# A hand-ordered first batch in a fused relu² attention and ReGLU feed-forward kernel: a relu, three gates, an exchange and some matmul passes change places

## The chip, the cores and the metric

The kernel runs on one core of one Trainium2 chip. The metric is the device time of one execution in microseconds (us). Before the change it is 420.81 us, the median of three runs (419.86 to 421.45). One more execution was taken with the hardware profiler; all durations below are from that one.

## The reference

Eight batches, 12 heads, 448 positions, head size 64; all inputs and the output are float32.

```python
scores = (1/8) * q @ k.transpose(0, 1, 3, 2)          # per batch and head: 448 x 448
attn   = np.maximum(scores, 0) ** 2 / 448
x      = (attn @ v)                                   # to 3584 tokens x 768 (heads side by side)
out    = (np.maximum(x @ w_gate, 0) * (x @ w_val)) @ w_out   # 768 -> 1536 -> 768
```

The kernel computes in bfloat16 with float32 accumulation. All constant factors are put into the scale of the gate's relu.

## The kernel before, in words

**Engines.** TensorE (PE) does every product as groups of four 64x64 matmuls that work side by side, one *pass* (`mm4`, L80) of 448 columns. ScalarE (ACT) and VectorE (DVE) read the results in PSUM. GpSimd (POOL) does little but issue loads and stores; SyncE (SP) issues DMA transposes and a few stores. Every instruction is pinned to program order (`pin`), so each engine works through its own queue in exactly the order in which the kernel text issues. An instruction that waits holds all that stand behind it on its engine.

**PSUM.** Eight banks, used in pairs. Score tiles and values take pairs 0 and 2 (`sc_later`, L193) or, in the first batch, 0, 2 and 4 in turn (`sc_first`). The FFN's sums take pairs 6 and 4 (`acc`). The first two FFN units of batch 0 have buffers of their own (`BEGUN_IN`, L349): pair 4 and pair 2. A buffer can be written again only when what read it is done.

**One batch of attention.** 21 score tiles, numbered n, seven for each of three *quads* of four heads (`tile_of`, L235). A tile is one pass. `relu2` (L223) then takes its 128x896 result: a relu on ACT from PSUM into a bfloat16 buffer `r_sb` (four buffers; L225), and a square on DVE (L226) into `attn`. When a quad's seven tiles are squared, seven *value passes* make its part of x (`value_passes`, L244), which is copied to x0. `exchange` (L251) then swaps the two halves of the partitions from x0 into x1, by two DVE copies.

**FFN.** `gv_unit` (L273): for each 128 of the 1536 hidden columns (index mf), 12 passes over x0 (e = 0) and x1 (e = 1), then a gate relu on ACT (L291) and a product on DVE (L292) into `hT`. `out_unit` (L309): 12 passes, added up and stored. From the second batch on, the score tiles of the next batch are laid between the passes of the FFN by hand-given places (unit, step) in `spread` and `evenly` (L458 to L472); three `transposes_event`s turn batch 1's q and k.

**The first batch** has no FFN to stand beside, and `first_batch` (L380) writes its order out by hand: some idle matmuls on zeros, the transposes of head pairs 0 and 1 (`first_transposes`), then the tiles. At n = 3, 5, 7, 9 two idle matmul pairs and the transposes of one more head pair follow the tile, each with a DVE copy from PSUM (`transposes`, L202); quad 1 needs head pairs 2 and 3. A tile's relu and square are issued two tiles later (`scored`). The values of quad 0 and 1 come after tile 12 and 17, with one DVE copy to x0 each (L415). Eight FFN passes (four for mf 0, four for mf 1) are done ahead of the last values; then come the exchanges, the copy of quad 2's x by ACT (L428), and the last 16 passes of mf 0 and 1. The regular FFN begins with mf 2.

**Loads** are all issued on POOL's queue, in the order of L363 to L376; a load is issued when the one eight places before it has landed. mf 0 and 1 use the weight chunk `gv0`, mf 2 to 5 `gv1`.

**End.** `out_pieces` (L330) writes the last 128 rows in three pieces, with their stores on the queues of POOL (2), SP (2), then ACT and SP (1 each), as L344 lists them.

Of the kernel before, what the change touches and what calls it, by code (L numbers as in the profile page):

```python
# [11 lines left out]
AF = mybir.ActivationFunctionType  # L12
# [4 lines left out]
def kernel(  # L17
# [22 lines left out]
    nc = tc.nc  # L40
# [28 lines left out]
    def pin(ins):  # L69
        return tc.keep_in_program_order(ins)  # L70
# [112 lines left out]
    def rotation(numbers):  # L183

        turn = [0]

        def take():
            n = numbers[turn[0] % len(numbers)]
            turn[0] += 1
            return banks[:, n:n + 2, :]  # L190
        return take

    sc_first, sc_later, acc = rotation((0, 2, 4)), rotation((0, 2)), rotation((6, 4))  # L193

    def transposes(b, hp, bank):

        ps = bank.bitcast(BF16).rearrange("p (t c) -> p t c", t=2)
        for t, nat in enumerate((kn_b[b % NB], qn_b[b % NB])):
            for i in range(4):
                for h2, half in HALVES:  # L200
                    pin(nc.tensor.transpose(ps[half, t, i * 128:i * 128 + 128], nat[:, 2 * hp + h2, i, :], ident))  # L201
        pin(nc.vector.tensor_copy(T_b[b % NB][:, :, hp, :], ps[:, :, 0:S]))  # L202
# [17 lines left out]
        for c in range(2):  # L220
            transposes(b, pair_of(b, 2 * qd + c), ps[:, c, :])

    def relu2(src, dst):  # L223
        r = rpool.tile([128, 2, S], BF16, name="r_sb")
        pin(nc.scalar.activation(r, src, AF.Relu))  # L225
        pin(nc.vector.tensor_tensor(dst, r, r, ALU.mult))  # L226

    attns = {}
# [1 line left out]
    def attn_of(b, qd):  # L230
        if (b, qd) not in attns:
            attns[b, qd] = atpool.tile([128, 2 * NC, S], BF16, name="attn")
        return attns[b, qd]

    def tile_of(b, n, ps):  # L235

        qd, i = divmod(n, NC)
        T = T_b[b % NB]
        a = i * 128 if i < 4 else (i - 4) * 128 + 64
        mm4([ps[:, r, :S] for r in range(2)], lambda r, c: T[:, 0, pair_of(b, 2 * qd + c), a:a + 64],  # L240
            lambda r, c: T[:, 1, pair_of(b, 2 * qd + c), :], True, True)
        return ps[:, :, :S], attn_of(b, qd)[:, 2 * i:2 * i + 2, :]

    def value_passes(b, qd, ps, i0, i1):  # L244

        attn, v_sb = attn_of(b, qd), v_b[b % NB]
        for i in range(i0, i1):
            mm4([ps[:, r, :S] for r in range(2)], lambda r, c: v_sb[:, 2 * qd + c, i, :],
                lambda r, c: attn[:, 2 * i + c, :], i == 0, i == NC - 1)

    def exchange(b, qd):  # L251
        a = slice(2 * qd, 2 * qd + 2)
        for (_, p), (_, other) in zip(HALVES, HALVES[::-1]):
            pin(nc.vector.tensor_copy(x_of[b][1][p, a, :], x_of[b][0][other, a, :]))  # L254

    def values(b, qd, ps):
        value_passes(b, qd, ps, 0, NC)
# [4 lines left out]
    def idle_matmuls(ps, n):  # L262

        for _ in range(n):
            mm2(ps[:, :S], blank[:, 0:128], blank, True, True)
# [4 lines left out]
    def new_x(b):  # L270
        x_of[b] = [xpool.tile([128, HP, S], BF16, name=f"x{n}") for n in range(2)]

    def gv_unit(b, mf, order, take):  # L273

        hT = hT_of[b - b % 2]
        c0 = CHUNK_OF[mf]
        w = gv_sb[c0]
        f = mf * 128 - CHUNKS[c0][0]
        col = (b % 2) * S
        o = []  # L280

        def step(n, e, hp):
            if n == 0:
                ps = take()
                o.extend(ps[:, r, :S] for r in range(2))
            x = x_of[b][e]
            mm4(o, lambda r, c: w[:, 2 * pair_of(b, hp) + (r ^ e), f + c * 64:f + c * 64 + 64], lambda r, c: x[:, hp, :],
                n == 0, n == H - 1)
            if n == H - 1:
                g_sb = gpool.tile([128, S], BF16, name="g_sb")  # L290
                pin(nc.scalar.activation(g_sb, o[0], AF.Relu, scale=float(out_scale)))  # L291
                pin(nc.vector.tensor_tensor(hT[:, mf, col:col + S], o[1], g_sb, ALU.mult))  # L292
        return [lambda n=n, e=e, hp=hp: step(n, e, hp) for n, (e, hp) in enumerate(order)]

# [9 lines left out]
    def store(b0, t, o_sb, c0, c1, engines):  # L304
        for s in range(2):
            pin(engines[s].dma_start(out=segment_rows(b0, 2 * t + s)[:, c0:c1],  # L306
                                     in_=o_sb[s * 64:s * 64 + 64, c0:c1]))
# [22 lines left out]
    def out_pieces(b0, t):  # L330

        hT = hT_of[b0]
        o_sb = opool.tile([128, d_model], FP32, name="o_sb")
        cuts = [0, OH, OH + OH // 2, d_model]
        turn = [acc(), acc()]
        for n, (c0, c1) in enumerate(zip(cuts, cuts[1:])):
            o_ps = turn[n % 2][:, n // 2, :c1 - c0]
            for kf in range(KF):
                mm2(o_ps, hT[:, kf, bass.ts(t, 128)], wo_sb[kf // 6][:, kf % 6, c0:c1], kf == 0, kf == KF - 1)
            if n == 2:  # L340
                pin(nc.vector.tensor_copy(o_sb[:, c0:c1], o_ps))  # L341
            else:
                pin(nc.scalar.activation(out=o_sb[:, c0:c1], in_=o_ps, func=AF.Copy))
            store(b0, t, o_sb, c0, c1, ((nc.gpsimd, nc.gpsimd), (nc.sync, nc.sync), (nc.scalar, nc.sync))[n])  # L344

    STRAIGHT = [(e, hp) for e in range(2) for hp in range(HP)]

    BEGUN = [(e, 2 * qd + c) for qds in (range(0, 2), range(2, 3)) for e in range(2) for qd in qds for c in range(2)]
    BEGUN_IN = (4, 2)  # L349

    def gv_units(b):
        b0 = b - b % 2
# [27 lines left out]
    def first_batch(units):  # L380


        def passes(u, n):
            for _ in range(n):
                units[u].pop(0)()

        def bank(n):
            return banks[:, n, :]

        def tile(n, at=None):  # L390
            todo.append(tile_of(0, n, sc_first() if at is None else banks[:, at:at + 2, :]))

        todo = []

        def scored():
            relu2(*todo.pop(0))

        idle_matmuls(bank(6), 12)
        first_transposes((6, 7, 5, 4))
        idle_matmuls(bank(2), 4)  # L400
        tile(0)
        tile(1)
        both = banks[:, 6:8, :]
        for n in range(2, 19):
            tile(n)
            if n in (3, 5, 7, 9):
                hp = n // 2 + 1
                idle_matmuls(bank(6 + hp % 2), 2)
                transposes(0, hp, bank(6 + hp % 2))
            if n in (12, 17):  # L410
                value_passes(0, n // 14, both, 0, NC)
            scored()
            if n in (12, 17):
                qd = n // 14
                pin(nc.vector.tensor_copy(x_of[0][0][:, 2 * qd:2 * qd + 2, :], both[:, :, :S]))  # L415
        tile(19)
        scored()
        passes(0, 4)
        scored()
        tile(20, 0)  # L420
        scored()
        value_passes(0, 2, both, 0, 4)
        scored()
        passes(1, 4)
        value_passes(0, 2, both, 4, NC)
        exchange(0, 0)
        exchange(0, 1)
        pin(nc.scalar.activation(x_of[0][0][:, 4:6, :], both[:, :, :S], AF.Copy))  # L428
        exchange(0, 2)
        for n in range(4):  # L430
            for u in range(2):
                passes(u, 2)

    def scores_event(b, n):
        return lambda: relu2(*tile_of(b, n, sc_later()))

    def values_event(b, qd):
        return lambda: values(b, qd, sc_later())

    def transposes_event(b, qd):  # L440
        return lambda: transpose_quad(b, qd)
# [16 lines left out]
    def spread(units, events):  # L458

        events = sorted(events, key=lambda e: e[:2])  # L460
        for u, unit in enumerate(units):
            for n, step in enumerate(unit):
                while events and events[0][:2] <= (u, n):
                    events.pop(0)[2]()
                step()
        assert not events

    def evenly(units, u0, u1, events):

        at = [(u, n) for u in range(u0, u1) for n in range(len(units[u]))]  # L470
        places = [at[int((i + 0.5) * len(at) / len(events))] for i in range(len(events))]
        return [(u, min(n, len(units[u]) - 4), e) for (u, n), e in zip(places, events)]  # L472
# [10 lines left out]
    units = units[2:] + [first[:8] + second[:8] + first[8:] + second[8:]] + more + out_units(0) + out_units(1)  # L483
    last = len(units) - 1
    todo = events_of(1)
    spread(units, [(2, 6, transposes_event(1, 0)), (2, 6, transposes_event(1, 1)), (2, 10, transposes_event(1, 2)),
                   (3, 0, todo.pop(0)), (10, 1, todo.pop())] + evenly(units, 3, 10, todo) +
           [(10, 7, values_event(1, 2)), (11, 0, lambda: new_x(2)),
            (13, 0, lambda: dma_transposes(2, 0)), (14, 6, lambda: dma_transposes(2, 1)),
            (19, 0, lambda: (hold(2), load_qk(3), load_v(3))), (last, 2, values_event(2, 2))] +  # L490
           evenly(units, 20, last - 1, events_of(2)) +
# [41 lines left out]
```

## Time and profile before

| what | us |
|---|---|
| median of three runs | 420.81 |
| the profiled execution | 420.87 |
| its span, first to last instruction | 419.1 |
| PE busy | 409.0 (98%) |
| DVE busy | 241.8 (58%) |
| ACT busy | 236.5 (56%) |
| relu of a score tile on ACT, 168 | 0.922 each |
| square on DVE, 168 | 0.624 each |
| gate relu on ACT, 96 | 0.543 each |
| exchange copy on DVE, 48 | 0.388 each |

The busy share of PE is an average. In the page's 40 slices of 10.5 us, PE has 7 and 8 tenths in the first two, in the second of which ACT has 9 and DVE 8; from the third on PE has 9 in all but the last, which has 5. A row of the timeline gives the start, the time from the first start to the last end, the engine, the line, what is written and read, and how many instructions were merged ("x8"); in brackets stands the idle time of the engine before it and what ended it.

### The profile page before, as it was taken

Reading aid. Unit: us, or ns where it says so; the run is one execution under the profiler, and the core shown is the slowest. Engines: PE = TensorE matmul, PEld = TensorE weight load, DVE = VectorE, ACT = ScalarE, POOL = GpSimd, SP = SyncE. Lnnn points to the kernel's source line nnn. Section 1 sums busy time; section 2 is a strip of 40 time slices with the busy share of each in tenths; the row PEclk is TensorE's granted clock in tenths of the full one; section 3 lists DMA queues with packets and bytes.
Section 4 is the critical chain, followed back from the end, with each engine's and each line's share of the span. In section 5 each row is a group of like instructions: output and inputs, shape, how many; then the busy total and the mean of one; then the engine's idle time right before and its main releaser. Section 6 shows DMA issues by size and latency. Waiting matters only on the chain.

```text
span 419.1 us, 19286 instructions
## 1 busy us (share of the span) xinstructions
PE 409.0 (98%) x8856; PEld 351.6 (84%) x8856; DVE 241.8 (58%) x424; ACT 236.5 (56%) x345; POOL 89.5 (21%) x147
## 2 busy tenths in 40 slices
PE   7899999999999999999999999999999999999995
PEld 3467677789989998899988999899988999889984
DVE  4885885437765766557555666556655565642221
ACT  4961884247765665565664756656665756622221
POOL 7923510024226100250023400260011000010012
PEclk9999999999999999999999999999999999999999
DMA  9999999359956960399323991289403100130014
GB/s 154 170 202 196 200 208 176 69 75 183 223 114 115 176 123 2 78 174 137 66 50 90 179 134 40 62 127 167 97 21 98 41 2 4 39 80 3 2 42 115
DMA packets 84338, 44.34 MB, mean 106 GB/s; under 512 B 54304, under 2 KB 82496, under 8 KB 84256
## 3 DMA queue, kind: packets, MB, share of 16 engines
q0 software_dynamic: 49600, 34.19, 52.6%
q1 hardware_dynamic: 34304, 8.67, 13.3%
q8 instruction: 69, 1.13, 1.1%
q10 hardware_dynamic: 352, 0.25, 0.2%
q14 instruction: 13, 0.11, 0.1%
HBM read 47.19 MB, written 11.01 MB: 139 GB/s over the span
## 4 chain that ended last, share of the span: by engine, by line
PE 93%; DVE 3%; DMA 1%; POOL 1%; ACT 1%; issue 0%; POOLq 0%; ACTq 0%
PE ps L73 92%; DVE attn L226 2%; DMA qn<-in_q_dram 1%; DVE kqT L202 1%; PE ps L201 1%; ACT r_sb L225 1%; POOL qn L116 0%; POOL kn L116 0%; DVE x L415 0%; DVE hT L292 0%; ACT g_sb L291 0%; DVE o_sb L341 0%; POOL ident L112 0%; POOLq L112 0%; ACTq L225 0%
## 5 line engine op out<-in xcount | busy, mean ns | idle before, releaser
L73 PE MATMUL ps<-x,gv 64*64 64x448 bf16 x4608 | 242.8, 349 | 0.7 <-ACT r_sb L225 0.3
L73 PEld LDWEIGHTS <-gv 64*64 64x64 bf16 x4608 | 193.8, 107 | 30.3 <-issue 2.7
L225 ACT ACTIVATE r_sb<-ps 128x896 bf16<-128x896 f32 x168 | 151.4, 922 | 51.0 <-PE ps L73 45.7
L226 DVE TENSOR_TENSOR attn<-r_sb 128x896 bf16<-128x896 bf16 x168 | 103.7, 624 | 77.7 <-ACT r_sb L225 77.0
L73 PE MATMUL ps<-wo,hT 64*64 64x384 bf16 (+2 forms) x2664 | 124.8, 321 | 0.2 <-issue 0.2
L73 PEld LDWEIGHTS <-hT 64*64 64x64 bf16 (+1 forms) x2664 | 105.5, 107 | 11.8 <-issue 1.1
L292 DVE TENSOR_TENSOR hT<-ps,g_sb 128x448 bf16<-128x448 f32 x96 | 59.7, 622 | 50.4 <-ACT g_sb L291 49.6
L291 ACT ACTIVATE g_sb<-ps 128x448 bf16<-128x448 f32 x96 | 52.1, 543 | 64.7 <-PE ps L73 60.7
L306 POOL DMA_DIRECT2D out_dram<-o_sb x56 | 29.7, 536 | 263.5 <-DVE o_sb L325 262.3
L73 PE MATMUL ps<-kqT 64*64 64x448 bf16 x672 | 75.7, 351 | 2.6 <-ACT r_sb L225 2.1
L73 PEld LDWEIGHTS <-kqT 64*64 64x64 bf16 x672 | 34.2, 107 | 9.3 <-issue 4.2
L325 DVE TENSOR_TENSOR o_sb<-ps,o_sb 128x384 f32<-128x384 f32 x54 | 29.9, 554 | 18.3 <-ACT o_sb L324 18.2
L324 ACT ACTIVATE o_sb<-ps 128x384 f32<-128x384 f32 x54 | 26.4, 488 | 24.8 <-PE ps L73 24.3
L73 PE MATMUL ps<-attn,vn 64*64 64x448 bf16 x672 | 38.6, 350 | 0.0
L73 PEld LDWEIGHTS <-vn 64*64 64x64 bf16 x672 | 28.5, 107 | 4.4 <-issue 0.3
L116 POOL DMA_DIRECT2D vn<-in_v_dram x36 | 23.8, 701 | 19.4 <-PE ps L73 8.0
L258 ACT ACTIVATE x<-ps 128x448 bf16<-128x448 f32 x21 | 11.4, 543 | 28.4 <-PE ps L73 28.4
L259 DVE CAST x<-ps 128x448 bf16<-128x448 f32 x21 | 13.1, 625 | 14.3 <-PE ps L73 14.3
L254 DVE COPY x<-x 64x896 bf16<-64x896 bf16 x48 | 18.6, 388 | 2.7
L116 POOL DMA_DIRECT2D qn<-in_q_dram x20 | 14.6, 761 | 1.1 <-POOLq L517 0.8
L116 POOL DMA_DIRECT2D kn<-in_k_dram x16 | 12.2, 776 | 0.8 <-DVE attn L226 0.5
L73 PE MATMUL ps<-blank 128*64 128x448 bf16 x48 | 7.4, 447 | 1.2 <-DVE blank L88 1.2
(35 smaller groups left out, 57.8 us busy)
## 6 DMA issues: line engine op xcount, KB each, us to landing
out_dram<-o_sb POOLq DMA_DIRECT2D x54, 192.0 KB, 3.6
kn<-in_k_dram POOLq DMA_DIRECT2D x7, 384.0 KB, 5.9
qn<-in_q_dram POOLq DMA_DIRECT2D x7, 384.0 KB, 8.3
vn<-in_v_dram POOLq DMA_DIRECT2D x14, 192.0 KB, 10.1
wo<-in_moe_w_out_dram POOLq DMA_DIRECT2D x2, 1152.0 KB, 16.8
kn<-in_k_dram POOLq DMA_DIRECT2D x7, 288.0 KB, 7.0
qn<-in_q_dram POOLq DMA_DIRECT2D x7, 288.0 KB, 9.9
vn<-in_v_dram POOLq DMA_DIRECT2D x14, 144.0 KB, 10.2
```

Source lines behind the costliest of these rows:

```text
L73: pin(nc.tensor.matmul(o, lhsT=l, rhs=r, start=start, stop=stop, skip_group_check=True))
L116: pin(nc.gpsimd.dma_start(out=o, in_=i))
L225: pin(nc.scalar.activation(r, src, AF.Relu))
L226: pin(nc.vector.tensor_tensor(dst, r, r, ALU.mult))
L254: pin(nc.vector.tensor_copy(x_of[b][1][p, a, :], x_of[b][0][other, a, :]))
L258: pin(nc.scalar.activation(x_of[b][0][:, 2 * qd, :], ps[:, 0, :S], AF.Copy))
L259: pin(nc.vector.tensor_copy(x_of[b][0][:, 2 * qd + 1, :], ps[:, 1, :S]))
L291: pin(nc.scalar.activation(g_sb, o[0], AF.Relu, scale=float(out_scale)))
L292: pin(nc.vector.tensor_tensor(hT[:, mf, col:col + S], o[1], g_sb, ALU.mult))
L306: pin(engines[s].dma_start(out=segment_rows(b0, 2 * t + s)[:, c0:c1], in_=o_sb[s * 64:s * 64 + 64, c0:c1]))
L324: pin(nc.scalar.activation(state[t][:, m], o[0], AF.Copy))
L325: pin(nc.vector.tensor_tensor(state[t][:, m], o[1], state[t][:, m], ALU.add))
```

## The change

- **A relu on DVE.** Tile 1's relu moves from ACT to DVE (`tensor_scalar_max`, from PSUM). It stays where it was issued: after tile 3, the transposes of head pair 2 and their copy.
- **Values sooner.** The values of quad 0 come after tile 11 (was 12), of quad 1 after tile 16 (was 17).
- **An exchange by DMA.** Quad 0's exchange is two DMAs on SP's queue, issued right after its copy to x0.
- **A third score buffer.** Tiles up to 14 take pairs 0, 2, 4 in turn; from tile 15 on they take 0 and 2, so that pair 4 is free for mf 0 from tile 17 on. mf 1 takes pair 0. Twelve FFN passes are done ahead of the last values, not eight: two after tile 17, two after tile 18, four after the first values of quad 2, and four more after tile 20's relu.
- Quad 2's copy to x0 is split between ACT and DVE; two idle matmul pairs after `first_transposes`, not four.
- **Gates.** In batch 0 the gate relus of mf 6, 8 and 10 move to DVE.
- **Places.** Batch 1's transposes and tiles begin later in the FFN of batch 0 and are spread over six units, not seven.
- **Last stores.** The second store of the second piece moves from SP to POOL.

```diff
-    def relu2(src, dst):
+    def relu2(src, dst, engine=nc.scalar):
         r = rpool.tile([128, 2, S], BF16, name="r_sb")
-        pin(nc.scalar.activation(r, src, AF.Relu))
+        if engine is nc.scalar:
+            pin(nc.scalar.activation(r, src, AF.Relu))
+        else:
+            pin(engine.tensor_scalar_max(r, src, 0.0))
         pin(nc.vector.tensor_tensor(dst, r, r, ALU.mult))
...
-            pin(nc.vector.tensor_copy(x_of[b][1][p, a, :], x_of[b][0][other, a, :]))
+            new, old = x_of[b][1][p, a, :], x_of[b][0][other, a, :]
+            pin(nc.vector.tensor_copy(new, old) if queue is None else queue.dma_start(out=new, in_=old))
...
-                pin(nc.scalar.activation(g_sb, o[0], AF.Relu, scale=float(out_scale)))
+                if b == 0 and mf >= 6 and mf % 2 == 0:
+
+                    pin(nc.vector.tensor_scalar(out=g_sb, in0=o[0], scalar1=float(out_scale), scalar2=0.0,
+                                                op0=ALU.mult, op1=ALU.max))
+                else:
+                    pin(nc.scalar.activation(g_sb, o[0], AF.Relu, scale=float(out_scale)))
...
-            store(b0, t, o_sb, c0, c1, ((nc.gpsimd, nc.gpsimd), (nc.sync, nc.sync), (nc.scalar, nc.sync))[n])
+            store(b0, t, o_sb, c0, c1, ((nc.gpsimd, nc.gpsimd), (nc.sync, nc.gpsimd), (nc.scalar, nc.sync))[n])
...
-    BEGUN_IN = (4, 2)
+    BEGUN_IN = (4, 0)
...
+        def buffer_of(n):
+            at = 2 * (n % 3) if n < 15 else 2 - 2 * (n % 2)
+            return banks[:, at:at + 2, :]
...
+        def scored(n):
+            relu2(buffer_of(n)[:, :, :S], attn_part(0, n), nc.vector if n == 1 else nc.scalar)
...
-        idle_matmuls(bank(2), 4)
+        idle_matmuls(banks[:, 2, :], 2)
         tile(0)
         tile(1)
-        both = banks[:, 6:8, :]
-        for n in range(2, 19):
+        for n in range(2, 17):
             tile(n)
             if n in (3, 5, 7, 9):
                 hp = n // 2 + 1
-                idle_matmuls(bank(6 + hp % 2), 2)
-                transposes(0, hp, bank(6 + hp % 2))
-            if n in (12, 17):
-                value_passes(0, n // 14, both, 0, NC)
-            scored()
-            if n in (12, 17):
-                qd = n // 14
-                pin(nc.vector.tensor_copy(x_of[0][0][:, 2 * qd:2 * qd + 2, :], both[:, :, :S]))
+                idle_matmuls(banks[:, 6 + hp % 2, :], 2)
+                transposes(0, hp, banks[:, 6 + hp % 2, :])
+            if n in (11, 16):
+                values_of(n // 16)
+            scored(n - 2)
+            if n in (11, 16):
+                copied(n // 16)
+            if n == 11:
+                exchange(0, 0, nc.sync)
+        scored(15)
+        tile(17)
+        passes(2, 0)
+        scored(16)
+        tile(18)
+        passes(2, 0)
+        scored(17)
         tile(19)
-        scored()
-        passes(0, 4)
-        scored()
-        tile(20, 0)
-        scored()
+        scored(18)
+        tile(20)
+        scored(19)
         value_passes(0, 2, both, 0, 4)
-        scored()
-        passes(1, 4)
+        passes(4, 1)
+        scored(20)
+        passes(2, 0, 1)
         value_passes(0, 2, both, 4, NC)
-        exchange(0, 0)
         exchange(0, 1)
-        pin(nc.scalar.activation(x_of[0][0][:, 4:6, :], both[:, :, :S], AF.Copy))
+        pin(nc.scalar.activation(x_of[0][0][:, 4, :], both[:, 0, :S], AF.Copy))
+        pin(nc.vector.tensor_copy(x_of[0][0][:, 5, :], both[:, 1, :S]))
         exchange(0, 2)
-        for n in range(4):
-            for u in range(2):
-                passes(u, 2)
+        for _ in range(3):
+            passes(2, 0, 1)
...
-    spread(units, [(2, 6, transposes_event(1, 0)), (2, 6, transposes_event(1, 1)), (2, 10, transposes_event(1, 2)),
-                   (3, 0, todo.pop(0)), (10, 1, todo.pop())] + evenly(units, 3, 10, todo) +
-           [(10, 7, values_event(1, 2)), (11, 0, lambda: new_x(2)),
+    spread(units, [(3, 4, transposes_event(1, 0)), (3, 4, transposes_event(1, 1)), (3, 8, transposes_event(1, 2)),
+                   (3, 10, todo.pop(0)), (10, 2, todo.pop())] + evenly(units, 4, 10, todo) +
+           [(10, 8, values_event(1, 2)), (11, 0, lambda: new_x(2)),
```

`passes(n, u, ...)` now takes n passes from each named unit in turn; `values_of` and `copied` are the two steps that stood in the loop.

## The prediction

> **What bounds the kernel now.** I read the page first, for the engine that is full:
>
> ```profile
> PE 409.0 (98%) x8856; PEld 351.6 (84%) x8856; DVE 241.8 (58%) x424; ACT 236.5 (56%) x345; POOL 89.5 (21%) x147
> PE   7899999999999999999999999999999999999995
> ```
>
> PE is full from the third slice on, so an edit pays only if it takes work from PE, closes gaps in PE's first 30 us, or shortens the tail behind the last matmul. A busy row hides short gaps, because an isolated pass is drawn 0.38 us long and back to back passes start 0.19 us apart (16 matmuls, four passes, last 0.95). So I read PE's waits in the first batch next, the window from 8 to 28 us:
>
> ```profile
> PE ps L73 <- ACT r_sb L225: 2.5, 6, 0.6
> ACT r_sb L225 <- PE ps L73: 0.9, 2, 0.8
> ```
>
> PE waits for ACT's relus, and ACT hardly waits: its chain of relus is the bound there. The timeline shows its pace, and the place where the change cuts in:
>
> ```profile
> 10.79 0.41 PE L201 MATMUL ps<-ident,qn 128*64 128x128 bf16 x8 [0.42 <-DMA qn<-in_q_dram]
> 11.13 0.57 PE L73 MATMUL ps<-kqT 64*64 64x448 bf16 x8
> 11.24 0.62 DVE L202 COPY kqT<-ps 128x896 bf16<-128x896 bf16 x1 [1.37 <-PE ps L201]
> 11.78 1.15 DVE L226 TENSOR_TENSOR attn<-r_sb 128x896 bf16<-128x896 bf16 x2
> ...
> 19.17 1.09 DVE L415 CAST x<-ps 128x896 bf16<-128x896 f32 x1
> ```
>
> The reader is to see three things. Head pair 2's q lands near 10.7; the transposes and their DVE copy follow. Tiles 4 and 5 start on PE at 11.13, at once. And DVE's square of tile 1 waits behind that copy until 11.78. ACT's starts, from narrow windows: tile 4 at 11.57, tile 20 at 24.93, mostly 0.80 apart; 16 steps of 0.80 are 12.8 of those 13.36 us, so 0.56 is gaps.
>
> **Step 1: tile 1's relu on DVE, the deciding one.** ACT has one relu fewer: -0.80 on its chain, if nothing else moves. But DVE's queue has the new relu behind head pair 2's copy, so it starts at 11.78. No row shows a relu on DVE. Its nearest row is the copy from the same float32 PSUM shape, 1.09 (L415); the low end is 0.62 (L202, 896 elements of bfloat16). I take 1.09: done at 12.87. Tile 4 writes pair 2, which tile 1 held (4 and 1 have the same rest by 3), and in the changed order its first matmul waits for DVE. It starts at 12.92 instead of 11.13, **+1.79** (low end +1.3). Queued behind it on PE are tile 5, the idle pairs, head pair 3's transposes and tile 6. ACT, done with tile 3 near 10.8, has nothing until 12.92 + 0.43 (tile 0: PE at 7.86, ACT at 8.29) = 13.35, against 11.57: **+1.78**. From tile 4 on ACT has the same 17 relus as before. So the one saved lies ahead of the hole, where it saves nothing. The two idle pairs left out (4 matmuls, 0.37) also lie ahead of it: 0, the DMA covers them.
>
> **Step 2: from the relus to mf 2.** With the same gaps (bounds 0 and twice 0.56) all relus come 1.8 later. Tile 18's starts at 23.33 before (two steps of 0.80 ahead of 24.93), so at 25.13, and ends at 26.05; tile 20 needs its buffer and starts at 26.10. From there PE has tile 20, 4 value passes, 4 FFN, 4 FFN, 3 value passes and 12 FFN: 28 x 0.19 = 5.32, so mf 2 starts at 31.42, plus about 0.2 for the last square and exchanges. Before, mf 2's gate started at 33.00, so its last pass at 32.57 and its first, 11 x 0.19 earlier, at 30.48. Difference **+1.1**, which has the four passes begun sooner in it (-0.76) and the DVE exchanges that no longer stand at the end:
>
> ```profile
> 26.71 2.48 DVE L254 COPY x<-x 64x896 bf16<-64x896 bf16 x6
> ```
>
> PE had some 0.5 of waits there. Bounds +0.5 (0.62 relu, all gaps closed, less the four passes) and +1.9 (the begun passes win nothing). Values one tile sooner, and the split copy of quad 2: 0, since ACT's chain ends later than they do; if that cover went, they would save parts of the same 0.5.
>
> **Step 3: exchange by DMA.** Quad 0's copy ends near 21 (after tile 11 instead of 12, -0.8, in a chain +1.8, from 20.26). SP starts the second DMA 0.83 later, as its last three stores are spaced. Landing after issue: 2.3 (the stores), 4.6 (SP's first k load, beside other loads), 5.9 (SP transposes at 103 to 117 us beside loads): 24.1 to 27.7. Its readers stand 9 passes behind tile 20, at 27.8. I take 0. Its 0.23 MB at some 190 GB/s delay the loads by 1.2: `gv1` lands at 28.7 (the load eight places later is issued then), so 29.9, still ahead of mf 2 at 31.4; batch 1's q at 36.2, so 37.4, ahead of its transposes, which move back by some 20 passes.
>
> **Step 4: mf 2 to mf 13.** 19 tiles and two values lie over 6 units instead of 7. Per unit PE needs 12 x 0.19 + 3.2 x 0.19 + 14/6 x 0.19 = 3.3. ACT needs 3.2 x 0.80 + half a gate (three of six move) 0.27 + copies 0.18 = 3.0; DVE 3.2 x 0.55 + 0.62 + half a gate at 0.63 (L259) 0.31 + values and exchange 0.47 = 3.2. PE still ends last, narrowly. Its waits there, read as steps beyond 0.19, are some 1.2 us before; I take 0, bounds -0.5 (the transposes no longer meet a load that lands at 36.15) and +0.7 (DVE blocks once per unit).
>
> **Step 5: the tail.**
>
> ```profile
> 414.02 2.16 SPq L306 DMA_DIRECT2D out_dram<-o_sb  x3
> 414.66 0.36 DVE L341 COPY o_sb<-ps 128x192 f32<-128x192 f32 x1 [3.10 <-PE ps L73]
> 415.04 0.54 ACTq L306 DMA_DIRECT2D out_dram<-o_sb  x1
> ```
>
> SP's third store starts at 415.66 only because two stand ahead of it; with one ahead it starts when DVE is done, 415.07: -0.59. POOL's added store starts at 414.5 and lands by 417.7 at the slowest row (3.2), against 417.9 before. I take **-0.4** (bounds -0.6, -0.1).
>
> **Sum.** +1.1 + 0 + 0 - 0.4 = +0.7, and +0.1 for the first-batch gaps, which I expect a little wider: +0.8. The profiled execution took 420.87 (span 419.1 and 1.77 around it), 0.06 over the median of the runs. Forecast **421.7**, no measurable change by the bound of 0.5% (2.1 us), about what a measurement of this kernel can tell from none. Bounds together: -0.6 and +2.5, so 420.2 to 423.3.
>
> **A rule and a row on the clock.** After the last matmuls the granted clock falls:
>
> ```profile
> 414.00:417.00 3.00, 0.61 (x16) 0.40 (x10) 0.36 (x1) 0.00 (x0) 0.50 (x1) 1.00 0.63 181
> 417.00:419.00 2.00, 0.00 (x0) 0.00 (x0) 0.00 (x0) 0.00 (x0) 0.00 (x0) 0.69 0.05 12
> ```
>
> It held for about 3 us without matmuls and then fell. PE's new hole, from 11.13 to 12.92, is 1.8 us; PE's longest hole before in the batch was about 0.9, at a clock of 1.00. The Trainium skill, "TensorE: Matmul & The Clock Gate", Part 1, has the clock halve after an idle window of about 3.4 us; by that the hole is short enough, and the trace agrees with its size.
>
> **Rivals.**
>
> *A: slower, the exchange DMA comes late.* It shares the DMA engines with loads that are queued deep: batch 1's k and q, issued at 15.8 to 18, took 14.7 to 17.9 to land. If the exchange needs over 6.0 from its issue at 21.8, PE stands still at 27.8 with everything behind it. At 8 us: +2.0, so **423.7**; at 14.7, +8.7. For: DMA is at 9 tenths there. Against: SP's own transfers beside loads landed in 4.6 and 5.9. The Trainium skill, "DMA: Bandwidth & Descriptors", Queues, rings and completion order, says that a DMA engine takes queues in turn, packet by packet; by that rule the deep queue doesn't hold the exchange, which no run here shows yet. Chance 0.15.
>
> *B: slower, the clock falls in the hole.* A window that is already partly idle (PE is sparse from 8 us) could end inside it. Then the next 3.4 us run at half pace: tiles, idle pairs and transposes of some 2.6 us take 5.2 where ACT needs 3.2, +2.0: **423.7**. Chance 0.05.
>
> *C: faster, the hole isn't paid.* If tile 1's relu were done before tile 4 needs it, ACT's chain would end 0.8 sooner, the four passes and the exchange would win up to 0.76, the tail 0.4: **418.9**. That is what the edit says it does. It speaks against this that the DVE queue holds the relu behind a copy that waits for a DMA; even a landing 2 us sooner leaves square, copy and relu in line (9.24 + 0.55 + 0.54 + 1.09 = 11.4). Chance 0.10.
>
> **How the numbers follow.** Forecast 0.70, A 0.15, B 0.05, C 0.10. Over 0.5% faster (below 418.7) is half of C: 0.05. Over 0.5% slower (above 422.9) is A, B and the forecast's upper end, 0.05: 0.25. Same: 0.70. The range takes the bounds, and reaches into A and B and towards C: 419.7 to 424.0.
>
> **What would show it.** In the changed trace: a gap on PE up to about 12.9 that ends with the DVE relu, and one on ACT from 10.8 to 13.3 (step 1); the last tile's relu near 26.7 and mf 2's gate near 34 (step 2); SP's exchange landing before 27.8, and no PE wait for it (step 3; else A); PE waits of about 1.2 us from 31 to 72 (step 4); SP's last store at some 0.6 after the one before it ends, and a span end 4.0 rather than 4.4 after the last matmul (step 5); a clock of 1.00 from 8 to 30 (else B). Wrong would be: no hole at tile 4, a DVE relu much under 1 us, or ACT or DVE becoming the bound in step 4.

## The result, and the profile after

The changed kernel takes 422.43 us (median of ten runs, 421.6 to 423.95), the kernel before 420.46 beside it: ratio 1.0047, 95% interval 1.0031 to 1.0063, so about 2.0 us slower, inside the bound of 0.5%. The profiled execution took 423.24 (span 421.4), 2.37 more than that of before. Its page, first lines and slices of PE:

```profile
span 421.4 us, 19282 instructions
PE 409.7 (97%) x8852; PEld 348.3 (83%) x8852; DVE 244.0 (58%) x427; ACT 233.6 (55%) x341; POOL 90.0 (21%) x148
PE   8799999999999999999999999999999999999995
```

PE's busy time grew by 0.7 us only, so most of the 2.3 us by which the span grew is idle time. I looked for it in the three places where PE has gaps. The first is the first batch; PE's waits there, from 8 to 28 us (total, times, longest):

```profile
ACT r_sb L226 <- PE ps L73: 2.7, 3, 2.0
PE ps L73 <- ACT r_sb L226: 2.1, 4, 0.6
PE ps L73 <- DVE r_sb L228: 1.7, 1, 1.7
```

The last row is new: one wait of 1.7 us for a relu on DVE (L228). The timeline around it:

```profile
10.78 0.62 DVE L202 COPY kqT<-ps 128x896 bf16<-128x896 bf16 x1 [0.76 <-PE ps L201]
11.32 1.08 DVE L228 TENSOR_SCALAR r_sb<-ps 128x896 bf16<-128x896 f32 x1
12.45 0.57 PE L73 MATMUL ps<-kqT 64*64 64x448 bf16 x8 [1.72 <-DVE r_sb L228]
12.93 2.54 ACT L226 ACTIVATE r_sb<-ps 128x896 bf16<-128x896 f32 x3 [1.96 <-PE ps L73]
```

DVE's relu stands behind head pair 2's copy; PE starts tile 4 when it is done (this is the hole of step 1), and ACT, idle for 1.96 us, follows. ACT's relu of tile 4 starts at 12.93 against 11.57, the last tile's at 26.47 against 24.93, the gate of mf 2 at 34.20 against 33.00: **+1.2**.

From there to the last DVE copy (L354, at 416.20) the changed kernel needs 0.34 us more than the kernel before. A gap of PE grew by about as much, from 0.17 to 0.54; the chain of work that ended last shows it in time order:

```profile
71.68 46.06 PE ps L73 x1021
117.74 0.54 issue
118.28 295.92 PE ps L73 x6537
```

("issue": PE waited for nothing that the profile shows. Before has 0.17 at 110.75.) The rest is the tail, 4.44 us from the last DVE copy to the span's end before and 5.2 after, **+0.76**. Its timeline in after:

```profile
415.00 1.56 POOL L319 DMA_DIRECT2D out_dram<-o_sb  x3 [0.56 <-ACT o_sb L356]
415.21 0.33 ACT L356 ACTIVATE o_sb<-ps 128x192 f32<-128x192 f32 x1 [0.50 <-PE ps L73]
415.56 1.54 SPq L319 DMA_DIRECT2D out_dram<-o_sb  x2
416.20 0.36 DVE L354 COPY o_sb<-ps 128x192 f32<-128x192 f32 x1 [3.10 <-PE ps L73]
```

SP's last store does come sooner: its two end at 417.10, 0.90 after the copy's start, where before its three ended 1.52 after it. The instructions of the program's last line show why that doesn't count (minimum/median/longest in ns, then first and last start). First after, then before:

```profile
L555 SPq EVENT_SEMAPHORE  x11: 17/28/1447, 417.2 to 421.3; - x11
L555 POOLq DRAIN  x3: 46/93/4672, 415.9 to 421.1; - x3
L555 SPq DRAIN  x3: 7/7/13, 419.3 to 420.9; - x3
```

```profile
L528 SPq EVENT_SEMAPHORE  x11: 17/28/28, 416.2 to 419.0; - x11
L528 POOLq DRAIN  x3: 46/102/4429, 413.9 to 418.8; - x3
L528 SPq DRAIN  x3: 7/7/13, 418.2 to 418.6; - x3
```

POOL closes with a drain of its queue, right behind its last store, of 4.43 us before (413.9 to 418.3) and 4.67 after (415.9 to 420.6). Before, SP had its stores back at 418.2, so the two ended together, POOL 0.1 later. After, SP is ready at 419.3, 3.1 after the last copy instead of 3.5, and waits 1.45 us for POOL: with its third store, POOL's drain begins 0.3 ahead of the last copy, not 0.8. The drain is in no row of busy time or of waits: the tail must be read in the last line's own instructions.

So by the two profiles: 1.2 + 0.34 + 0.76 = 2.3.

### The profile page after: what moved, and what is told of

Its sections match the earlier page's. It is cut to its first block, busy times and chain, and to the rows that moved or that the text cites. A ratio compares the mean times of both kernels' runs of the same rounds, so it can differ in the third digit from the quotient of the medians.

```text
span 421.4 us, 19282 instructions
## 1 busy us (share of the span) xinstructions
PE 409.7 (97%) x8852; PEld 348.3 (83%) x8852; DVE 244.0 (58%) x427; ACT 233.6 (55%) x341; POOL 90.0 (21%) x148
## 3 DMA queue, kind: packets, MB, share of 16 engines
q8 instruction: 69, 1.13, 1.1%
## 4 chain that ended last, share of the span: by engine, by line
PE 93%; DVE 3%; ACT 1%; DMA 1%; issue 0%; POOL 0%; POOLq 0%; DVEq 0%; ACTq 0%
PE ps L73 91%; DVE attn L229 1%; DMA kr<-in_k_dram 1%; PE ps L201 1%; ACT r_sb L226 1%; DVE kqT L202 1%; PE ps L210 0%; DVE x L418 0%; DVE r_sb L228 0%; POOL out_dram L319 0%; DVE x L262 0%; DVE kn L128 0%; DVE hT L305 0%; DVE x L456 0%; ACT g_sb L304 0%
## 5 line engine op out<-in xcount | busy, mean ns | idle before, releaser
L73 PEld LDWEIGHTS <-hT 64*64 64x64 bf16 (+1 forms) x2664 | 102.4, 107 | 14.1 <-issue 1.4
L304 ACT ACTIVATE g_sb<-ps 128x448 bf16<-128x448 f32 x93 | 50.5, 544 | 60.4 <-PE ps L73 56.4
L73 PE MATMUL ps<-kqT 64*64 64x448 bf16 x672 | 74.5, 351 | 4.1 <-ACT r_sb L226 2.1
L73 PEld LDWEIGHTS <-kqT 64*64 64x64 bf16 x672 | 33.2, 106 | 12.0 <-issue 6.8
```

Source lines behind the costliest of these rows:

```text
L73: pin(nc.tensor.matmul(o, lhsT=l, rhs=r, start=start, stop=stop, skip_group_check=True))
```

## The experiments

Theory: the hole costs the first batch, POOL's drain the tail. Rivals: hole or tail is absorbed somewhere, or the tail hangs on the stores' landing. In the table, "gate" is the start of the third gate relu (mf 2), "copy" that of the last DVE copy, "tail" from there to the span's end, "gaps" are PE's "issue" gaps behind the first batch (of the kind explained under e8), all in us of one profiled execution. Spans are given to 0.1 us, so a tail is good to 0.05.

| run | ratio to before | gate | copy | tail | gaps |
|---|---|---|---|---|---|
| before | | 33.00 | 414.66 | 4.44 | 0.17 |
| after | 1.0047 [1.0031, 1.0063] | 34.20 | 416.20 | 5.2 | 0.54 |
| e1_relu_on_act | 1.0020 [1.0004, 1.0036] | 32.11 | 414.28 | 5.12 | 0.36, 0.69 |
| e2_tail_back | 1.0046 [1.0024, 1.0067] | 35.06 | 415.93 | 4.57 | none |
| e3_before_tail | 1.0016 [0.9999, 1.0032] | 32.44 | 414.41 | 4.89 | 0.56 |
| e4_relu_early | 1.0024 [1.0006, 1.0041] | 32.17 | 414.65 | 5.15 | 1.08 |
| e5_before_hole | 1.0035 [1.0015, 1.0056] | 34.31 | 415.24 | 4.46 | none |
| e6_tail_all_pool | 1.0053 [1.0032, 1.0075] | 32.47 | 415.95 | 6.65 | 0.29, 0.25, 1.08 |
| e7_tail_hw | 0.9977 [0.9962, 0.9992] | 32.69 | 413.83 | 3.57 | 0.18 |
| e8_act_tail_hw | 0.9993 [0.9974, 1.0013] | 32.52 | 414.73 | 3.87 | 0.38, 0.70 |
| e9_act_hw_v_later | 0.9962 [0.9948, 0.9976] | 32.00 | 413.51 | 3.79 | 0.67 |
| e10_before_hw_v_later | 0.9969 [0.9954, 0.9984] | 33.26 | 414.70 | 3.8 | none |
| e11_act_exchange_dve | 1.0006 [0.9992, 1.0021] | 32.77 | 413.64 | 4.86 | none |

The five kernels with the first batch of before have their gate between 32.44 and 33.26, so differences of a few tenths there mean little.

### The hole alone

**e1_relu_on_act**: after, with tile 1's relu on ACT.

```diff
-            relu2(buffer_of(n)[:, :, :S], attn_part(0, n), nc.vector if n == 1 else nc.scalar)
+            relu2(buffer_of(n)[:, :, :S], attn_part(0, n), nc.scalar)
```

> The changed kernel with tile 1's relu back on ACT, all else as changed. Theory (the hole): tile 4 is held on PE from 10.7 to 12.45 by the relu on DVE, and this alone turns the first batch from a gain into a loss. Without it the first batch is that of the kernel before with four passes (0.76 us) begun sooner and its exchange copies out of the way: mf 2's first pass at about 29.8 (30.5 before, 31.7 in the changed kernel), so 1.6 to 1.9 us less than the changed kernel, about +0.2 (0 to +0.5) against the kernel before, all of it from the tail. Rival (the order of the begun passes, the third buffer or the DMA exchange cost the time): PE waits elsewhere in the first batch, mf 2 not before 31.2, under 0.5 us gained.

**e5_before_hole**: before, with only that relu on DVE.

```diff
...
-            relu2(*todo.pop(0))
+            relu2(*todo.pop(0), nc.vector if len(taken) == 1 else nc.scalar)
...
```

(`relu2` takes the engine as it does in after; `taken` counts the calls.)

> The kernel before with one edit, tile 1's relu on DVE where it stood. Theory (the hole): tile 4 waits for it on PE to about 12.9 instead of 11.1, ACT has a gap of some 2 us ahead of tile 4's relu, and with no passes begun sooner to make up for it the third gate of the FFN comes 1.4 to 1.9 later (33.0 before): +1.4 to +1.9 us against the kernel before. Rival (a relu fewer on ACT pays for the hole): +0.5 or less.

E1's gate comes 2.1 sooner than after's, e5's 1.3 later than before's. In time, e1 is 0.0027 under after (the two ratios' difference, 1.1 us, where 1.6 to 1.9 was expected), e5 1.0035 over before (1.5 us): the hole by itself makes before slower, by most of what the whole change costs. E1 kept less than its gate promised, and the chain of its run shows where some of it went:

```profile
41.35 2.77 PE ps L73 x56
44.12 0.36 issue
44.48 24.17 PE ps L73 x496
...
69.89 40.30 PE ps L73 x868
110.19 0.69 issue
```

**e4_relu_early**: after, with tile 1's relu issued right behind tile 3, ahead of the copy that waits for a DMA.

```diff
             tile(n)
+            if n == 3:
+                scored(1)
...
-            scored(n - 2)
+            if n != 3:
+                scored(n - 2)
```

> The changed kernel with tile 1's relu and square on DVE issued ahead of the idle pairs and transposes that follow tile 3, so ahead of head pair 2's copy in DVE's queue. Theory (it is the place in DVE's queue, not the relu on DVE): DVE starts the relu when tile 0's square is issued, near 9.9, and is done near 11.0; tile 4 starts behind the transposes at about 11.1 with no hole, ACT has one relu less behind it, mf 2 begins at about 29.5: some 2.2 us less than the changed kernel, 0.3 less than with the relu on ACT, and -0.1 (-0.5 to +0.3) against the kernel before, with the tail's loss still in it. Rival (a relu on DVE is dear in itself, as DVE is busy 22 of 24 us there): not better than with the relu on ACT, or worse by 0.5 and more.

The hole is gone, yet the time is e1's, where I expected a little less. DVE's queue in e4:

```profile
9.58 1.08 DVE L228 TENSOR_SCALAR r_sb<-ps 128x896 bf16<-128x896 f32 x1
10.70 0.63 DVE L229 TENSOR_TENSOR attn<-r_sb 128x896 bf16<-128x896 bf16 x1
11.24 0.62 DVE L202 COPY kqT<-ps 128x896 bf16<-128x896 bf16 x1
```

and in e1:

```profile
10.53 0.62 DVE L202 COPY kqT<-ps 128x896 bf16<-128x896 bf16 x1 [0.78 <-PE ps L201]
11.07 1.15 DVE L229 TENSOR_TENSOR attn<-r_sb 128x896 bf16<-128x896 bf16 x2
```

The relu of 1.08 us keeps DVE busy up to head pair 2's copy, which comes 0.7 later than in e1; some 0.3 of that is q, whose transposes run later in this execution (10.36 against 10.08). What takes the gain is on ACT. Its tile 4 in e4:

```profile
11.20 4.39 ACT L226 ACTIVATE r_sb<-ps 128x896 bf16<-128x896 f32 x5 [0.57 <-PE ps L73]
```

ACT, with one relu less behind it, waits 0.57 for PE's tile 4, which stands behind those transposes and so behind q's load. It starts the tile only 0.18 sooner than in e1 (11.38), and after some shorter waits its last tile's relu comes at 24.76 against 24.59. So the relu that ACT is spared is no gain, early or late.

### The tail alone

**e2_tail_back**: after, with the last stores as before. **e3_before_tail**: before, with after's last stores.

```diff
-((nc.gpsimd, nc.gpsimd), (nc.sync, nc.sync), (nc.scalar, nc.sync))[n]
+((nc.gpsimd, nc.gpsimd), (nc.sync, nc.gpsimd), (nc.scalar, nc.sync))[n]
```

(e3; e2 is the reverse.)

> The changed kernel with the last stores as before (POOL's added store back on SP). Theory (POOL's closing drain): after its last store POOL sits in a drain of 4.4 to 4.7 us, and the end waits for it; with one store fewer on POOL the drain starts 0.53 sooner after the last matmul: the span from the last DVE copy's start to the end goes from 5.2 back to 4.4 to 4.5, 0.6 to 0.8 us less than the changed kernel. Rival (the tail's 0.76 is chance of one execution): no change within 0.2, or 0.4 more, as SP's third store comes 0.6 later.

> The kernel before with only the last stores changed (one of SP's goes to POOL). Theory (POOL's closing drain): +0.5 to +0.7 us, the span from the last DVE copy's start to the end 5.0 to 5.2 instead of 4.4. The prediction's step 5, as a rival: -0.4 us. Rival (chance): 0 within 0.2.

The tail follows the stores both ways, -0.63 and +0.45. E3's time is +0.7 us, with an interval that just reaches no change; e2's time is not below after's, and its interval, 0.4% wide, can't tell 0.6 us. So a pair that pushes harder, both on before: **e6_tail_all_pool**, the last rows' six stores all on POOL, and **e7_tail_hw**, none on POOL.

```diff
e6: ((nc.gpsimd, nc.gpsimd), (nc.gpsimd, nc.gpsimd), (nc.gpsimd, nc.gpsimd))[n]
e7: ((nc.sync, nc.scalar), (nc.sync, nc.scalar), (nc.scalar, nc.sync))[n]
```

> The kernel before with all six of the last piece's stores on POOL. Theory (POOL's closing drain): POOL issues four more stores, the last pair after the last DVE copy, 0.53 each, so it is done near 2.0 after that copy's start, and drains 4.4 to 4.7 from there: the end is 6.8 to 7.3 after the last copy's start instead of 4.4, +2.4 to +2.9 us. Rival (the stores' landing sets the end, 2.4 to 3.2 for POOL): the end is 1.5 + 3.2 + 1.1 = 5.5 to 6.0 after it, +1.1 to +1.6.

> The kernel before with none of the last piece's stores on POOL (first and second piece on SP and ACT, one each). Theory: POOL's last store is that of the unit before, so its drain ends 1.1 earlier and no longer matters; SP's last store starts right after the last copy, at 0.4 instead of 1.0, lands 2.3 later, and the end follows 1.1 later: 3.9 after the last copy's start instead of 4.4, -0.5 us (-0.2 to -0.7). Rival (ACT's two added issues of 0.54 delay its copies of the second piece): 0 to +0.5.

The last instructions of e6, then of e7:

```profile
L528 POOLq DRAIN  x3: 46/93/4771, 417.1 to 422.4; - x3
L528 SPq DRAIN  x3: 7/7/13, 420.2 to 422.1; - x3
```

```profile
L528 POOLq DRAIN  x3: 46/93/5217, 411.5 to 417.2; - x3
L528 SPq DRAIN  x3: 7/7/13, 416.5 to 416.9; - x3
```

E6's last four stores landed 1.8 us after issue (median; 2.1 to 2.7 in before and after), the last at 419.2, and still its tail is the longest, 6.65 (6.8 to 7.3 was expected, 5.5 to 6.0 by the rival): landing alone doesn't set it, POOL's drain from 417.1 to 421.9 does. But the drain itself follows POOL's own landing: in twelve of the thirteen traces it ends 1.77 to 1.95 us behind the landing of POOL's last store, in e6 2.7 behind it. E7 lets POOL go at 411.5 and its tail falls to 3.57, more than the 0.5 expected, with drain and SP together again (416.7 and 416.5). The times agree: 1.0053 and 0.9977. (E6's profiled execution, at 424.41, lies 1.6 above the median of its runs; its tail is read within it.)

### Where the first batch's gain goes

**e8_act_tail_hw**: e1 with e7's stores.

> The changed kernel with tile 1's relu back on ACT and none of the last piece's stores on POOL: the parts of the change that pay, and a shorter tail. Theory: third gate of the FFN near 32.1 (33.0 before), -0.8; tail -0.5; together -0.9 to -1.4 us against the kernel before. Rival (what the first batch wins is lost later, to PE's waits near 110 us): 0 to -0.5.

By e1's gain over before at the gate it should lie under e7, and it does not: gaps of 0.38 and 0.70 stand at 44.53 and 110.64. What are these? The windows from the start to a point inside the gap count PE's matmuls ahead of it (the second figure's "x"; e3 at 105.2, e1 at 110.5, after at 118.0):

```profile
0.00:105.20 105.20, 100.07 (x2011) 70.81 (x2012) 68.20 (x123) 62.07 (x87) 38.90 (x63) 1.00 1.16 168
```

```profile
0.00:110.50 110.50, 105.83 (x2139) 75.89 (x2140) 73.08 (x132) 64.67 (x91) 40.34 (x65) 1.00 1.16 170
```

```profile
0.00:118.00 118.00, 111.82 (x2267) 80.85 (x2268) 78.32 (x140) 68.14 (x95) 41.25 (x67) 1.00 1.13 167
```

2011, 2139, 2267: steps of 128 matmuls, or 256 instructions with their weight loads. The gaps at 44 us in e1, e8 and e9 stand behind 732 matmuls, 11 x 128 below 2139 but for one missing record, and all thirteen gaps of the table lie on this grid. (E10 has one of 0.28 at 92 us that does not, and it stays unexplained.) The page's DMA table gives queue q8, kind instruction, 69 packets and 1.13 MB: 16 KB each, and PE's 17,704 instructions over 69 are 257 for one. So each gap stands where PE comes to a new packet of its own program. From the records of q8 and of PE's starts:

| packet due at matmul | landed | PE ran on at | previous packet begun | landed after that |
|---|---|---|---|---|
| after, 2267 | 117.00 | 118.28 | 112.08 | 4.9 |
| e1, 732 | 43.16 | 44.49 | 38.56 | 4.6 |
| e1, 2139 | 109.32 | 110.89 | 104.69 | 4.6 |
| e9, 2139 | 105.38 | 110.10 | 104.79 | 0.6 |

In the thirteen gaps the packet landed 4.1 to 5.4 us after PE began the one before it, and PE uses one up in about 6. In all of them PE runs on 1.3 to 1.6 us after the landing; at the 195 packet boundaries between 36 and 125 us in the thirteen traces it never runs on sooner than 1.26 after one, and where it has no gap as much as 5 us lie between. So PE waits for its own instructions there: that is read from the place and time of the gaps, as the profile names no releaser. The gaps matter: from the gate to the last copy the thirteen executions differ by 2.6 us (380.87 to 383.48), and with the table's gaps taken off by 1.0 (380.84 to 381.86). **e9_act_hw_v_later** is e8 with the load of batch 3's v moved from unit 19 to unit 30, out of that stretch; **e10_before_hw_v_later** makes the same move in e7.

```diff
-            (19, 0, lambda: (hold(2), load_qk(3), load_v(3))), (last, 2, values_event(2, 2))] +
+            (19, 0, lambda: (hold(2), load_qk(3))), (30, 0, lambda: load_v(3)), (last, 2, values_event(2, 2))] +
```

> E8 (relu on ACT, none of the last piece's stores on POOL) with batch 3's load of v moved from unit 19 to unit 30 of the FFN, behind the DMA transposes of batch 3. Theory (a wall in time): near 110 us PE waits for something that keeps its own time, its instructions on a queue of the same DMA engines that q, k, v and SP's transposes fill; the kernels that reach that stretch early wait there most (E1 0.69, E8 0.70, E4 1.08; the kernel before 0.17, E5 none), so the win of the first batch is given back. With less load beside the transposes the gap at 105 to 118 us goes from 0.7 to 0.2 or less, and the time is 0.5 to 0.8 under E8, 0.8 to 1.2 under the kernel before. Rival (the gap belongs to that place in PE's own instructions, or is chance): a gap of 0.5 and more remains there, and the time is E8's within 0.3.

> E7 (the kernel before with none of the last piece's stores on POOL) with batch 3's load of v moved in the same way. Theory (a wall in time): this kernel comes to that stretch 0.3 later and waits 0.2 there, so 0 to -0.2 us against E7, -0.9 to -1.2 against the kernel before. Rival (the load of v costs PE or SP time in itself): 0.4 and more faster than E7.

In the stretch around the gap (length; PE, PEld, DVE, ACT, POOL busy; clock, DMA share, GB/s), e8 and then e9. The DMA share adds up the times of all packets, and can pass 1:

```profile
102.00:108.00 6.00, 6.00 (x149) 4.92 (x141) 5.47 (x10) 3.59 (x6) 1.20 (x2) 1.00 1.40 211
108.00:114.00 6.00, 5.30 (x129) 4.49 (x125) 3.53 (x6) 4.50 (x7) 1.04 (x2) 1.00 1.14 227
```

```profile
102.00:108.00 6.00, 6.00 (x150) 4.96 (x144) 5.28 (x10) 3.81 (x6) 1.20 (x2) 1.00 0.71 153
108.00:114.00 6.00, 6.00 (x152) 5.01 (x148) 4.33 (x8) 5.33 (x9) 1.05 (x2) 1.00 0.93 145
```

With the v load gone DMA's share falls from 1.40 to 0.71, the packet lands 0.6 after the one before was begun, and PE has no gap. **E9 is the fastest version, 419.12 us, 0.9962 [0.9948, 0.9976], and beats both kernels.** The move is worth 0.0031 on e8, 1.3 us where 0.5 to 0.8 was expected. In the two profiles e9 takes 0.70 less from the gate to the last copy (381.51 against 382.21), as much as the gap that is gone, though its gap at 44 us is 0.29 longer; the other 0.5 lies ahead of the gate, where the two kernels are the same. On e7 the move is worth only 0.0008, less than can be told, as e7 had only 0.18 to lose there. E9 and e10 can't be told apart either, so what the changed first batch is worth without its hole stays open; it is small.

**e11_act_exchange_dve**: e1, with quad 0's exchange on DVE again.

```diff
-                exchange(0, 0, nc.sync)
+                exchange(0, 0)
```

> E1 (the changed kernel with tile 1's relu on ACT) with quad 0's exchange back on DVE, at the place where the DMA was issued. It tells what the DMA is worth. Theory: two copies of 0.39 stand in DVE's queue in the middle of the squares, where DVE has no idle time (5.87 of 6 us from 20 to 26), so the last square and with it the last values come 0.8 later; PE has 0.2 of other work there: third gate of the FFN near 32.9 instead of 32.1, +0.5 to +0.8 us against E1. Rival (DVE has slack that the page doesn't show): within 0.2 of E1.

The gate comes 0.66 later, as expected for two DVE copies in the chain, but the time is no longer than e1's (1.0006 against 1.0020): e11 has no packet gap where e1 has 1.05 us of them. What the DMA exchange wins is lost again to them; part of that is likely chance, as the intervals overlap. Moving a load away from the gap at 44 us was not tried.

## Why the prediction held, and where it failed

No change over 0.5% was forecast and none came; the time is 0.7 over the forecast and inside its range. That it lies there owes something to luck, as one term had the wrong sign and one cost stood in no term. By its steps, which added up to +0.8 against a measured +2.0:

- **Step 1, the hole.** Right. Relu 1.08 (taken 1.09); PE's wait 1.72, forecast 1.79; tile 4 at 12.45 instead of 12.92, only because q landed some 0.5 sooner in this execution.
- **Step 2, to mf 2.** Right in mechanism and, in this pair, in size: +1.2 against +1.1. The size is in part luck: e2, with the same first batch but a second ACT wait of 0.86 at tile 6, has its gate 0.9 later still, 2.1 over before and so just beyond the bound of +1.9. Against the mean of the five kernels with the first batch of before (32.77), after and e2 lie 1.9 later and e1, e8 and e9, which have no hole, 0.6 sooner. So the hole costs this gate some 2 us, and the other edits give back about 0.6. Rival C, the hole not paid, did not occur; and its 418.9 was too low in any case, as e1, which has no hole, takes 421.22 and is not faster than before.
- **Step 3, the exchange.** Right, narrowly. DMA in the window from 19 to 28 us (queues, then KB each and us from issue to landing):

```profile
q0 software_dynamic: 1836, 1.67, 115.5%
q1 hardware_dynamic: 160, 0.23, 8.2%
gv<-in_moe_w_gate_dram POOLq DMA_DIRECT2D x2, 384.0 KB, 18.2
gv<-in_moe_w_val_dram POOLq DMA_DIRECT2D x1, 384.0 KB, 19.1
x<-x SPq DMA_DIRECT2D x2, 112.0 KB, 6.1
```

  The loads of q0 took 18 to 19 us, SP's exchange 6.1, and no PE wait names it; rival A's 8 us did not come. The rule of the Trainium skill on which I set A's chance ("DMA: Bandwidth & Descriptors", Queues, rings and completion order: an engine takes its queues in turn by packets) agrees with that. The second landed near 27.8, just when its readers came.
- **Step 4, mf 2 to 13.** Right: from the gate of mf 2 to the wait for hT near 71 us, 37.48 against 37.62 before, where 0 was taken.
- **Step 5, the tail: the step that failed.** "I take -0.4 (bounds -0.6, -0.1)"; it was +0.76. The part on SP came as worked out (its last store 0.62 sooner, SP ready some 0.4 sooner), and the added store did land in time. But I took the end for the last store's landing and did not read the end's other leg, POOL's drain. In before it already ended 0.1 behind SP, so that an earlier last store on SP could win next to nothing, and a later last store on POOL moved the end. From -0.4 to +0.76 is 1.16 us, nearly all of the 1.2 that the sum lacks against the medians; against the two profiles (+2.3) it lacks 1.5, and the next term is the gaps.
- **The sum** had no term for the packet gaps, +0.37 here. That PE waits in a busy stretch for its program was in before's chain, as 0.17 of "issue" at 110.75, and I passed over it.
- **Rival B** did not occur: the clock was 1.00 through the hole (8 to 12.4 us, and on to 30).

## What to carry to other kernels

Before a store is moved to another queue at the end of a program, read each engine's closing instructions, not only the stores' landings: what ends beside the engine that is made faster bounds the gain, and here POOL's drain ended with SP within 0.1 us. When a relu is moved to another engine, look at what stands ahead of it in the new queue: here that was a copy waiting for a load, so the relu's buffer came free late, and PE stood still for 1.7 us. And where PE is full and DMA is full as well, time won earlier can be lost to the arrival of PE's own program, so a load moved out of that stretch can be worth as much as work saved.

## What the runs showed of the hardware

- POOL's closing drain took 4.4 to 5.4 us in all thirteen traces (4.43 before, 4.67 after, 4.77 e6, 5.22 e7, 5.40 e9), counted from behind its last store. It is longer where that store has 192 KB and lands later (3.4 us after issue in e7, 2.5 for the 48 KB of before), and except in e6 it ended 1.77 to 1.95 us behind that landing. What it waits for inside is not shown.
- PE's program arrives in packets of 16 KB (69 in a run), and each lands 0.6 us after the one before was begun where DMA has room (e9 at 105 us; the median behind 200 us of after is 0.8), but 4.1 to 5.4 in the thirteen gaps, with a DMA share of 1.4 around e8's; the waits were 0.17 to 1.08 us. The Trainium skill, "Runtime: NRT & Kernel Launch", Instruction fetch mechanics, has the same blocks of 256 instructions and calls the cost of crossing into a new one mostly hidden. The traces agree on the size (257 PE instructions for each packet), and show that under full DMA it is not always hidden.
